# Linear attention and a gated MLP on one core: the order of the readers of the key banks, the time at which even query rows are sent, and the number of output buffers

## The chip, the cores and the metric

The kernel runs on one core of a Trainium2 chip. The metric is the device time of one execution in microseconds (us), taken as the median over runs. A core has five engines that run their own instruction streams in order and wait for each other by semaphores: TensorE (PE in the profile, with its weight loads as PEld), VectorE (DVE), ScalarE (ACT), GpSimd (POOL) and SyncE (SP), which here only starts transfers. Transfers run on 16 DMA engines and are started from SP's, POOL's or ACT's queue.

## The reference

Two stages follow each other. The inputs are q, k, v of shape 8 x 8 x 576 x 64 (batch, heads, tokens, head size), a feature matrix w_phi of 64 x 128, and the weights of a gated MLP.

```python
def phi(x):
    proj = np.einsum('bhsd,df->bhsf', x, w_phi)
    proj = proj - np.max(np.abs(proj), axis=-1, keepdims=True)
    return np.concatenate([np.exp(proj), np.exp(-proj)], axis=-1)
q_p, k_p = (phi(q), phi(k))
kv = np.einsum('bhsf,bhsd->bhfd', k_p, v)
z = np.sum(k_p, axis=2)
num = np.einsum('bhsf,bhfd->bhsd', q_p, kv)
den = np.einsum('bhsf,bhf->bhs', q_p, z)[..., None] + 1e-06
x = num / den            # then heads side by side: 8 x 576 x 512

h = np.maximum(x @ w_in, 0.0)                 # 512 -> 1024, halves u and v
v_n = (v - mean(v)) / sqrt(var(v) + 1e-06)    # over the 512 columns of v
v_s = w_spatial @ v_n + b_spatial             # mixes the 576 tokens
out = (u * v_s) @ w_out
```

Each key row needs the exponential of its 128 projections with both signs, and the largest absolute projection of the row. The kernel takes exp(proj) and exp(-proj) of the plain projections, and carries the maximum into the sums by scaling v with exp(-max) and exp(max).

## The kernel before, in words

**Units.** Of a batch's 576 tokens, 512 are "main" tokens and 64 are a "tail". A unit of work is either a pair of heads of one batch with its 512 main tokens (four pairs a batch, 32 in all), or the 64 tail tokens of two batches with all heads (four units). There are 36 units; unit 0 is the first pair, unit 1 the first tail, units 9, 18 and 27 the other tails.

**Steps.** `step(i)` (line 608) writes one step of a software pipeline. In the order of the list ORDER it takes the keys of unit i (`a_keys`, then `a_scale`), its queries (`a_queries`), the attention of unit i-3, the sums of unit i-2 (`a_kv`), the transposed inputs of unit i+1 (`a_transpose`), the query features of unit i-2 (`a_qfeat`), the output of attention of unit i-4 (`a_x_t`) and the transposed query maxima of unit i-1 (`a_max_t`). Between them `fill` takes tasks of the second stage from a queue, as many as a credit of estimated TensorE time allows. When the last pair of a batch is done, `b_tasks` puts that batch's second stage into the queue. What is still in the queue after the last step runs behind it. The scheduler of the language then orders the instructions of each engine by these priorities and its own estimate of times; instructions wrapped in `pin` keep their written order among themselves.

**Keys (line 251).** `by_token` multiplies the transposed keys with w_phi into a bank of PSUM, the memory that TensorE writes: one bank of 128 x 512 numbers for each half of the unit. Of each bank VectorE takes the maxima (`mk`, one instruction of 128x4 from 128x512, line 259) and ScalarE the exponentials (`kf`, two instructions of 128x512, line 262). In the program's waits, an instruction that reads a bank and was written after another engine's reader of that bank waits for that reader. So the exponentials of a half wait for its maxima. `a_scale` (line 279) then takes the exponentials `em` of the maxima on ScalarE (two instructions of 128x8), and scales v by them on GpSimd (`vs`, two instructions of 128x512 and a small one; `vst` for the tails).

**Queries (line 264).** The same projection in two banks, and the maxima `mq` of both on VectorE. GpSimd (VectorE in the first five units) splits mq into a high and a low part `mhl`; a step later `a_max_t` (line 306) transposes that on TensorE. From batch 2 on (`merged`), VectorE puts the 16 transposed rows into the transposed queries themselves, so that one matmul takes projection and maximum together. The transposed queries `qT` of a pair hold odd heads in partitions 64 to 127 and even heads in partitions 0 to 63. The 16 rows of the maxima overwrite rows 0 to 15 for the odd heads; before that, `q_even` (line 223) has sent rows 0 to 63 to another tile `qE`, one of four that units take in turn, by a transfer from SP's queue. The first copy (line 311) waits for that transfer. A second copy (line 312) puts the maxima into `qE`.

**Transposed inputs.** From batch 2 on, `cross` transposes the keys and queries of a whole batch by two DMA transposes in SP's queue, two steps ahead of the batch's first pair.

**Second stage.** `b_v` and `b_ln` make the normalised v half (ScalarE relu, VectorE statistics, GpSimd normalisation `vn`), `b_u` the u half, `b_s` the mixing of tokens with the product on VectorE, `b_o` the last matmul. `o_mm` (line 524) evicts each 128x512 result into an output buffer `ob`, on VectorE and ScalarE in turn; SP sends it out. There are four such buffers, which the first two loads use too.

Of the kernel before, what the change touches and what calls it, by code (L numbers as in the profile page):

```python
# [8 lines left out]
FP32 = mybir.dt.float32  # L9
BF16 = mybir.dt.bfloat16  # L10
AF = mybir.ActivationFunctionType
ALU = mybir.AluOpType
AX = mybir.AxisListType
# [3 lines left out]
def kernel(  # L17
# [15 lines left out]
    nc = tc.nc  # L33

    B, H, S, D = q.shape
    F = w_phi.shape[1]
    DM = moe_w_in.shape[0]
    DFF = moe_w_in.shape[1]
    HALF = DFF // 2
    P = 128  # L40
    KC = DM // P
    NP = H // 2
    NB = 4
# [8 lines left out]
    a1 = ctx.enter_context(tc.tile_pool(name="stage_a", bufs=2))  # L52
    feat = ctx.enter_context(tc.tile_pool(name="feat", bufs=2))
    small = ctx.enter_context(tc.tile_pool(name="small", bufs=3))
    s2 = ctx.enter_context(tc.tile_pool(name="stage_b", bufs=2))
# [4 lines left out]
    def pin(start):  # L60
        return lambda *a, **kw: tc.keep_in_program_order(start(*a, **kw))

    def main_ap(t, b, h0=0, n=H):
        return bass.AP(tensor=t.tensor, offset=t.offset + (b * H + h0) * S * D,
                       ap=[[NB * D, P], [S * D, n], [1, NB * D]])
# [5 lines left out]
    st = {}  # L71
# [43 lines left out]
    alloc(0)  # L115
    first = {}
    for x, t in (("k", k), ("q", q)):
        first[x] = s2.tile([P, 2, NB * D], FP32, tag="ob", name="first", bufs=4)
        pin(nc.sync.dma_start)(out=first[x], in_=main_ap(t, 0, 0, 2))
    ident = cpool.tile([P, P], BF16)  # L120
    make_identity(nc, ident)
# [100 lines left out]

    def q_even(u):
        u["qE"] = qts[u["i"] % len(qts)]
        pin(nc.sync.dma_start)(out=u["qE"][0:D], in_=u["qT"][0:D])

    def a_transpose(u):
        src = st[u["b"]] if u["pair"] else gs[u["g"]]
# [15 lines left out]
    def by_token(xT, half):  # L244
        ps = psum.tile([P, 4, F], FP32, tag="bank", name="ps")
        for x in range(2):
            nc.tensor.matmul(out=ps[:, 2 * x:2 * x + 2, :], lhsT=xT[:, 2 * half + x, :], rhs=wphi2,  # L247
                             start=True, stop=True)
        return ps

    def a_keys(u):

        u["mk"] = small.tile([P, H], FP32, tag="mk", name="mk")
        u["kf"] = feat.tile([P, 2, H, F], BF16, tag="kf" if u["pair"] else "kf_t", name="kf",
                            bufs=4 if u["pair"] else 2)
        for half in range(2):
            pk = by_token(u["kT"], half)
            hs = slice(4 * half, 4 * half + 4)
            nc.vector.tensor_reduce(out=u["mk"][:, hs], in_=pk, axis=AX.X, op=ALU.max,  # L259
                                    apply_absolute_value=True)  # L260
            for s, sc in ((0, 1.0), (1, -1.0)):
                nc.scalar.activation(out=u["kf"][:, s, hs, :], in_=pk, func=AF.Exp, bias=0.0, scale=sc)  # L262

    def a_queries(u):

        m, early = mhl[u["i"] % NM], u["i"] < EARLY
        if not early:
            mq = small.tile([P, H], FP32, tag="mq", name="mq")
        for half in range(2):
            pq = by_token(u["qT"], half)  # L270
            if early and half == 0:
                mq = pq[:, 0, 0:H]
            nc.vector.tensor_reduce(out=mq[:, 4 * half:4 * half + 4], in_=pq, axis=AX.X, op=ALU.max,  # L273
                                    apply_absolute_value=True)
        eng = nc.vector if early else nc.gpsimd
        eng.tensor_copy(out=m[:, 0:H], in_=mq)
        eng.tensor_tensor(out=m[:, H:2 * H], in0=mq, in1=m[:, 0:H], op=ALU.subtract)

    def a_scale(u):
        em = small.tile([P, 2, H], FP32, tag="em" if u["pair"] else "em_t", name="em", bufs=3 if u["pair"] else 1)  # L280
        for s, sc in ((0, -1.0), (1, 1.0)):
            nc.scalar.activation(out=em[:, s, :], in_=u["mk"], func=AF.Exp, bias=0.0, scale=sc)  # L282
        if u["pair"]:
            pj = u["pj"]
            vs = feat.tile([P, 2, H, DA], BF16, tag="vs", name="vs", bufs=4)
            for s in range(2):
                nc.gpsimd.tensor_tensor(out=vs[:, s, :, 0:D], in0=st[u["b"]]["v"][:, pj * H:(pj + 1) * H, :],  # L287
                                        in1=em[:, s, :].unsqueeze(2).to_broadcast([P, H, D]), op=ALU.mult)
            nc.gpsimd.tensor_copy(out=vs[:, :, :, D:DA], in_=em.unsqueeze(3).to_broadcast([P, 2, H, 2]))
            u["vs"] = vs  # L290
        else:
            d = gs[u["g"]]
            d["vs"], d["unit"], d["em"] = vst[u["g"] % 2], u, em
            for bl in range(2 if u["i"] > 1 else 1):
                tail_scale(u["g"], bl)
# [70 lines left out]
    def norm(pn, x, r=slice(0, P)):  # L366
        n = r.stop - r.start
        rc = small.tile([P, 4, 1], FP32, tag="rc", name="rc", bufs=4)
        nc.vector.reciprocal(out=rc[r], in_=pn[r, :, D:D + 1])
        nc.vector.tensor_tensor(out=x, in0=pn[r, :, 0:D], in1=rc[r].to_broadcast([n, 4, D]), op=ALU.mult)  # L370
# [25 lines left out]
    def tail_num(g, bls):  # L396
        d = gs[g]
        qf = d["unit"]["qf"]
        if "xt" not in d:
            d["xt"] = a1.tile([P, H, D], BF16, tag="xt", name="xt")  # L400
        for i in range(2):
            pn = psum.tile([P, 4, DA], FP32, tag="bank", name="pn")
            for y in range(4):
                for bl in bls:
                    r = slice(bl * TL, (bl + 1) * TL)
                    for s in range(2):
                        nc.tensor.matmul(out=pn[r, y, :], lhsT=qf[i][:, s, y, r],
                                         rhs=st[2 * g + bl]["kv"][:, 4 * i + y, s, :],
                                         start=(s == 0), stop=(s == 1))
            r = slice(bls[0] * TL, (bls[-1] + 1) * TL)  # L410
            norm(pn, d["xt"][r, 4 * i:4 * i + 4, :], r)
# [73 lines left out]
    def b_u_tail(g, bls):  # L485
        d = gs[g]
        if "uTt" not in d:
            d["uTt"] = s2.tile([P, KC, P], BF16, tag="uTt", name="uTt")
        r = slice(bls[0] * TL, (bls[-1] + 1) * TL)
        pu = psum.tile([P, KC, P], FP32, tag="bank", name="pu")  # L490
        for dc in range(KC):
            for kc in range(KC):
                nc.tensor.matmul(out=pu[:, dc, r], lhsT=w_in_bf[:, kc, dc * P:(dc + 1) * P],
                                 rhs=d["xTt"][:, kc, r], start=(kc == 0), stop=(kc == KC - 1))
        nc.scalar.activation(out=d["uTt"][:, :, r], in_=pu[:, :, r], func=AF.Relu, bias=0.0, scale=1.0)
# [28 lines left out]
    def o_mm(lhs, r):  # L524
        po = psum.tile([P, DM], FP32, tag="bank", name="po")
        for dc in range(KC):
            nc.tensor.matmul(out=po[r], lhsT=lhs(dc), rhs=w_out_bf[:, dc, :], start=(dc == 0), stop=(dc == KC - 1))  # L527
        ob = s2.tile([P, DM], FP32, tag="ob", name="ob", bufs=4)
        turn[0] ^= 1
        (nc.vector.tensor_copy if turn[0] else nc.scalar.copy)(out=ob[r], in_=po[r])  # L530
        return ob
# [76 lines left out]
    def step(i):  # L608

        if i == 0:  # L610
            a_transpose(units[0])
        for what, share in ORDER:
            for u in units[max(0, i - 5):i + 2]:
                if u["i"] + lag(u, what) != i or (what in ("sums", "attention", "out") and not u["pair"]):
                    continue
                last = u["pair"] and u["pj"] == NP - 1
                if what == "keys":
                    a_keys(u)
                    a_scale(u)
                elif what == "sums":  # L620
                    a_kv(u)
                elif what == "queries":
                    a_queries(u)
                elif what == "next":
                    a_transpose(u)
                elif what == "maxima":
                    a_max_t(u)
                elif what == "out":
                    a_x_t(u)
                    if last:  # L630
                        finish_batch(u, tail_x_t)
                        queue.extend(b_tasks(u["b"]))
                elif what == "features":
                    a_qfeat(u)
                elif what == "attention":
                    a_num(u)
                    if last:
                        finish_batch(u, tail_num)
            fill(share)
# [12 lines left out]
    def at(i, f, *a):  # L652
        io.setdefault(i, []).append(lambda: f(*a))
# [22 lines left out]
    at(7, weights_with_max)  # L676
    for u in units:
        if merged(u):
            at(u["i"], q_even, u)
    for i in range(NU + 4):  # L680
        step(i)
        for f in io.get(i, []):
# [33 lines left out]
```

## Time and profile before

| what | value |
|---|---|
| median of 13 runs | 294.45 us (292.23 to 298.0) |
| the profiled execution's own time | 292.89 us |
| its span, first to last instruction | 291.1 us |
| its granted TensorE clock, mean | 0.987 |
| maxima of keys (line 259), VectorE | 72 instructions, 47.8 us busy |
| exponentials of keys (line 262), ScalarE | 144 instructions, 76.7 us busy |
| exponentials of maxima (line 282), ScalarE | 72 instructions, 13.1 us busy |
| scaled v (line 287), GpSimd | 64 instructions, 65.7 us busy |
| q_even transfers | 24, 64 KB each, 3.2 us to landing (median) |
| full output transfers | 32, 256 KB each, 2.7 us to landing (median) |

The profile gives the busy time of each engine, for groups of instructions by line, and for any stretch of the span. An instruction's own duration is longer than its share of the engine where instructions overlap: four exponentials in a row take 2.06 us from the first start to the last end, while each one lasts about 0.65 us. The waits list says which line stood still, for whose result, how often and how long. The chain of waits goes back from the last instruction through whatever released each step.

### The profile page before, as it was taken

To read this page: it belongs to the slowest core of one execution; us is meant where nothing else is said; L and a number is where in the kernel's file an instruction comes from. 1 tells how busy PE (TensorE), PEld (TensorE's weight loads), DVE (VectorE), ACT (ScalarE), POOL (GpSimd) and SP (SyncE) were. 2 spreads that over 40 slices of the span, in tenths; PEclk is the share of its full clock that TensorE was granted. 3 is DMA by queue.
4 is the path that set the end of the run, shared out by engine and by line. 5 is a ranking of instruction groups with operands and counts; after the bars stand their busy time and mean duration, and the time that the engine had idled before them with its cause. 6 is when DMAs were issued, how large, how long until landed. Compare 5 with 4: busy or idle time off the path is not lost.

```text
span 291.1 us, 7872 instructions
## 1 busy us (share of the span) xinstructions
PE 259.0 (89%) x2974; PEld 171.2 (59%) x2974; DVE 226.0 (78%) x552; ACT 220.4 (76%) x498; POOL 185.5 (64%) x332
## 2 busy tenths in 40 slices
PE   3188899999999799999699999999899989999983
PEld 2067676766656446666557666666566666545441
DVE  5389997966989928899778998888899976654641
ACT  7658998797689917999889787898998865666011
POOL 8579998886336696359879973766769530068100
PEclk9999999999999959999999999999999999999999
DMA  7979999945659299989991899999912005400036
GB/s 194 224 132 159 207 233 205 165 154 72 92 169 170 47 211 161 172 192 192 150 187 30 213 185 178 236 247 207 194 32 56 19 11 182 146 0 1 2 100 225
DMA packets 83626, 41.88 MB, mean 144 GB/s; under 512 B 50626, under 2 KB 78978, under 8 KB 83588
## 3 DMA queue, kind: packets, MB, share of 16 engines
q1 hardware_dynamic: 56100, 29.90, 45.6%
q0 software_dynamic: 27328, 11.41, 32.9%
q8 instruction: 23, 0.38, 0.6%
q14 instruction: 15, 0.12, 0.1%
q10 hardware_dynamic: 160, 0.07, 0.1%
HBM read 32.85 MB, written 9.44 MB: 145 GB/s over the span
## 4 chain that ended last, share of the span: by engine, by line
PE 46%; ACT 17%; DVE 16%; POOL 8%; DMA 7%; issue 4%; SPq 0%; DVEq 0%; POOLq 0%; ACTq 0%
PE ps L502 9%; PE po L527 8%; ACT kf L262 6%; PE pv L428 5%; ACT qf L346 5%; PE pu L481 4%; PE ps L247 4%; DMA q_tl<-in_q_dram 4%; DVE mk L259 4%; PE pv L359 3%; PE pn L379 3%; PE ps L503 2%; DVE mq L273 2%; DMA out_dram<-ob 2%; POOL vst L302 2%
## 5 line engine op out<-in xcount | busy, mean ns | idle before, releaser
L262 ACT ACTIVATE kf<-ps 128x512 bf16<-128x512 f32 x144 | 76.7, 651 | 9.1 <-DVE mk L259 8.7
L287 POOL TENSOR_TENSOR vs<-v_f,em 128x512 bf16<-128x512 f32 x64 | 65.7, 1048 | 27.9 <-ACT em L282 27.5
L346 ACT ACTIVATE qf<-pq 128x512 bf16<-128x512 f32 x128 | 66.9, 634 | 11.0 <-PE pq L325 8.1
L259 DVE TENSOR_REDUCE mk<-ps 128x4 f32<-128x512 f32 x72 | 47.8, 679 | 1.6 <-PE ps L247 0.7
L273 DVE TENSOR_REDUCE mq<-ps 128x4 f32<-128x512 f32 x62 | 40.1, 679 | 1.6 <-PE ps L247 1.4
L502 PE MATMUL ps<-w_spT,vn 128*128 128x512 bf16 x128 | 34.9, 392 | 2.7 <-POOL vn L445 2.4
L505 DVE TENSOR_TENSOR uT<-ps,uT 128x512 bf16<-128x512 f32 x32 | 21.7, 686 | 15.3 <-PE ps L503 15.3
L428 PE MATMUL pv<-w_in_bf,xT 128*128 128x512 bf16 x128 | 31.6, 379 | 0.6 <-DMA xT<-x 0.5
L481 PE MATMUL pu<-xT,w_in_bf 128*128 128x512 bf16 x128 | 31.4, 379 | 0.1
L527 PE MATMUL po<-w_out_bf,uT 128*128 128x512 bf16 x128 | 30.6, 379 | 0.0
L431 DVE BATCH_NORM_STATS2 stats<-vr 128x6 f32<-128x512 bf16 (+1 forms) x37 | 24.7, 682 | 5.8 <-ACT vr L430 5.5
L530 ACT COPY ob<-po 128x512 f32<-128x512 f32 (+1 forms) x18 | 10.5, 603 | 24.0 <-PE po L527 21.2
L379 PEld LDWEIGHTS <-qf 128*128 128x128 bf16 x512 | 21.0, 98 | 8.4 <-ACT qf L346 2.3
L359 PE MATMUL pv<-vs,kf 128*128 128x66 bf16 x512 | 25.1, 195 | 0.9 <-ACT kf L262 0.9
L430 ACT ACTIVATE vr<-pv 128x512 bf16<-128x512 f32 (+1 forms) x37 | 21.8, 627 | 5.4 <-PE pv L428 5.2
L370 DVE TENSOR_TENSOR x<-pn,rc 128x256 bf16<-128x256 f32 x64 | 24.7, 417 | 0.3
L379 PE MATMUL pn<-kv,qf 128*128 128x66 bf16 x512 | 23.3, 195 | 1.6 <-ACT qf L346 1.5
L445 POOL TENSOR_SCALAR vn<-vr,rs 128x512 bf16<-128x512 bf16 x32 | 24.2, 766 | 0.6
L359 PEld LDWEIGHTS <-kf 128*128 128x128 bf16 x512 | 22.4, 99 | 2.7 <-issue 1.9
L302 POOL TENSOR_TENSOR vst<-v_tl,em 64x512 bf16<-64x512 f32 x16 | 16.3, 1038 | 11.0 <-ACT em L282 10.7
L483 ACT ACTIVATE uT<-pu 128x512 bf16<-128x512 f32 x32 | 20.1, 644 | 3.1 <-PE pu L481 3.1
L361 PE MATMUL pv<-vst,kf 128*128 128x66 bf16 x128 | 21.5, 193 | 0.7 <-POOL vst L304 0.7
(128 smaller groups left out, 543.2 us busy)
## 6 DMA issues: line engine op xcount, KB each, us to landing
v_f<-in_v_dram SPq DMA_DIRECT2D x8, 1024.0 KB, 8.7
out_dram<-ob SPq DMA_DIRECT2D x32, 256.0 KB, 2.7
k_bf<-in_k_dram POOLq DMA_DIRECT2D x7, 512.0 KB, 6.7
q_bf<-in_q_dram POOLq DMA_DIRECT2D x7, 512.0 KB, 7.6
qt<-qT_b SPq DMA_DIRECT2D x24, 64.0 KB, 3.2
v_tl<-in_v_dram SPq DMA_DIRECT2D x8, 128.0 KB, 7.7
w_in_bf<-in_moe_w_in_dram POOLq DMA_DIRECT2D x2, 512.0 KB, 8.1
out_dram<-ob SPq DMA_DIRECT2D x8, 128.0 KB, 2.5
```

What stands on the lines that cost most here:

```text
L259: nc.vector.tensor_reduce(out=u["mk"][:, hs], in_=pk, axis=AX.X, op=ALU.max, apply_absolute_value=True)
L262: nc.scalar.activation(out=u["kf"][:, s, hs, :], in_=pk, func=AF.Exp, bias=0.0, scale=sc)
L273: nc.vector.tensor_reduce(out=mq[:, 4 * half:4 * half + 4], in_=pq, axis=AX.X, op=ALU.max, apply_absolute_value=True)
L287: nc.gpsimd.tensor_tensor(out=vs[:, s, :, 0:D], in0=st[u["b"]]["v"][:, pj * H:(pj + 1) * H, :], in1=em[:, s, :].unsqueeze(2).to_broadcast( ...
L346: nc.scalar.activation(out=qf[:, s], in_=pq, func=AF.Exp, bias=0.0, scale=sc)
L359: nc.tensor.matmul(out=pv[:, hh, s, :], lhsT=u["kf"][:, s, 4 * hh + c, :], rhs=u["vs"][:, s, 4 * hh + c, :], start=(c == 0), stop=False)
L370: nc.vector.tensor_tensor(out=x, in0=pn[r, :, 0:D], in1=rc[r].to_broadcast([n, 4, D]), op=ALU.mult)
L379: nc.tensor.matmul(out=pn[:, pos, :], lhsT=u["qf"][hh][:, s, pos, :], rhs=d["kv"][:, 2 * u["pj"] + hh, s, :], start=(s == 0), stop=(s == 1))
L428: nc.tensor.matmul(out=pv[r], lhsT=lhs(kc), rhs=w_in_bf[:, kc, HALF:DFF], start=(kc == 0), stop=(kc == KC - 1))
L481: nc.tensor.matmul(out=pu, lhsT=w_in_bf[:, kc, dc * P:(dc + 1) * P], rhs=d["xT"][:, kc, :], start=(kc == 0), stop=(kc == KC - 1))
L502: nc.tensor.matmul(out=ps, lhsT=d["vn"][:, sp, cs], rhs=w_spT[:, sp, 0:T0], start=(sp == 0), stop=False)
L527: nc.tensor.matmul(out=po[r], lhsT=lhs(dc), rhs=w_out_bf[:, dc, :], start=(dc == 0), stop=(dc == KC - 1))
```

## The change

Four things are changed.

1. **Order of the readers of the key banks.** Both banks are filled first. Then the program has the exponentials of half 0, the maxima of half 1, the exponentials of half 1, and the maxima of half 0. By the waits of the built program, the exponentials of half 0 wait for TensorE alone, the maxima of half 1 for TensorE alone, the exponentials of half 1 for the maxima of half 1, and the maxima of half 0 for the exponentials of half 0.
2. **`a_scale` goes from behind `a_keys` to behind `a_queries`** within the step, and so do its `em` and `vs`.
3. **`q_even` of the second, third and fourth pair of a batch is sent at the end of the step before.** It reads the batch's transposed queries directly.
4. **Five output buffers instead of four.** The tiles `xt` and `uTt` of the tails go from two buffers to one.

```diff
-        first[x] = s2.tile([P, 2, NB * D], FP32, tag="ob", name="first", bufs=4)
+        first[x] = s2.tile([P, 2, NB * D], FP32, tag="ob", name="first", bufs=5)
...
-        pin(nc.sync.dma_start)(out=u["qE"][0:D], in_=u["qT"][0:D])
+        pin(nc.sync.dma_start)(out=u["qE"][0:D], in_=st[u["b"]]["qT"][0:D, 4 * u["pj"]:4 * u["pj"] + 4, :])
...
-        for half in range(2):
-            pk = by_token(u["kT"], half)
-            hs = slice(4 * half, 4 * half + 4)
-            nc.vector.tensor_reduce(out=u["mk"][:, hs], in_=pk, axis=AX.X, op=ALU.max,
+        pk = [by_token(u["kT"], half) for half in range(2)]
+
+        def maxima(half):
+            nc.vector.tensor_reduce(out=u["mk"][:, 4 * half:4 * half + 4], in_=pk[half], axis=AX.X, op=ALU.max,
                                     apply_absolute_value=True)
+
+        def exponentials(half):
             for s, sc in ((0, 1.0), (1, -1.0)):
-                nc.scalar.activation(out=u["kf"][:, s, hs, :], in_=pk, func=AF.Exp, bias=0.0, scale=sc)
+                nc.scalar.activation(out=u["kf"][:, s, 4 * half:4 * half + 4, :], in_=pk[half], func=AF.Exp,
+                                     bias=0.0, scale=sc)
+
+        exponentials(0)
+        maxima(1)
+        exponentials(1)
+        maxima(0)
...
-            d["xt"] = a1.tile([P, H, D], BF16, tag="xt", name="xt")
+            d["xt"] = a1.tile([P, H, D], BF16, tag="xt", name="xt", bufs=1)
...
-            d["uTt"] = s2.tile([P, KC, P], BF16, tag="uTt", name="uTt")
+            d["uTt"] = s2.tile([P, KC, P], BF16, tag="uTt", name="uTt", bufs=1)
...
-        ob = s2.tile([P, DM], FP32, tag="ob", name="ob", bufs=4)
+        ob = s2.tile([P, DM], FP32, tag="ob", name="ob", bufs=5)
...
                     a_keys(u)
-                    a_scale(u)
...
                     a_queries(u)
+                    a_scale(u)
...
-            at(u["i"], q_even, u)
+            at(u["i"] - min(u["pj"], 1), q_even, u)
```

## The prediction, made before the changed kernel was run

> **What bounds the kernel now.** I read the page's busy times first, then busy time by stretch, the waits, and the timelines of VectorE and ScalarE around the keys of some units.
>
> ```profile
> PE 259.0 (89%) x2974; PEld 171.2 (59%) x2974; DVE 226.0 (78%) x552; ACT 220.4 (76%) x498; POOL 185.5 (64%) x332
> PE 46%; ACT 17%; DVE 16%; POOL 8%; DMA 7%; issue 4%; SPq 0%; DVEq 0%; POOLq 0%; ACTq 0%
> ```
>
> The first line is the busy time over the span of 291.1 us, the second the chain that ended last by engine. No engine is full, and the chain moves between four of them: every engine takes its work in a fixed order and waits for the others in turn. So I go by stretches (columns: length, then PE, PEld, DVE, ACT and POOL busy with counts, clock, DMA).
>
> ```profile
> 22.00:50.00 28.00, 24.65 (x361) 19.54 (x360) 26.04 (x75) 25.66 (x60) 26.58 (x42) 1.00 1.34 202
> 110.00:160.00 50.00, 45.91 (x578) 31.60 (x576) 42.14 (x106) 45.78 (x110) 35.74 (x65) 1.00 0.96 155
> 160.00:210.00 50.00, 48.47 (x591) 32.11 (x590) 45.20 (x102) 43.23 (x102) 35.30 (x61) 1.00 1.23 209
> 210.00:235.00 25.00, 24.54 (x290) 16.52 (x289) 24.11 (x55) 22.50 (x54) 17.67 (x35) 1.00 0.20 41
> 235.00:280.00 45.00, 43.09 (x418) 24.44 (x417) 27.02 (x64) 20.27 (x37) 14.01 (x27) 1.00 0.16 54
> ```
>
> Until 50 us VectorE and ScalarE are both above 90%; from 50 to 235 PE, VectorE and ScalarE share the load, and VectorE has 0.9 us free of the last 25; after 235 PE works off the queue alone. What the change goes for are these waits (total, times, longest):
>
> ```profile
> POOL vs L287 <- ACT em L282: 27.5, 13, 4.6
> ACT kf L262 <- DVE mk L259: 8.7, 8, 4.3
> DVE ob L530 <- DMA out_dram<-ob: 3.6, 3, 1.5
> ACT ob L530 <- DMA out_dram<-ob: 2.8, 2, 1.8
> DVE qT_b L311 <- DMA qt<-qT_b: 1.2, 2, 1.0
> ```
>
> ScalarE waits for the key maxima 8.7 us in all, 5.9 of them before 50 us. In 28 of 36 units it does not wait: it is late with older work when the bank is ready. Unit 5 is typical (VectorE, then ScalarE):
>
> ```profile
> 32.07 1.29 DVE L259 TENSOR_REDUCE mk<-ps 128x4 f32<-128x512 f32 x2
> 33.27 1.28 DVE L273 TENSOR_REDUCE mq<-ps 128x4 f32<-128x512 f32 x2
> ...
> 31.20 2.08 ACT L346 ACTIVATE qf<-pq 128x512 bf16<-128x512 f32 x4
> 33.11 2.13 ACT L262 ACTIVATE kf<-ps 128x512 bf16<-128x512 f32 x4
> ```
>
> VectorE has taken both maxima by 33.27, while ScalarE begins the exponentials at 33.11, straight after the features qf.
>
> **The change, part by part.** The sum is made against the profiled execution's own 292.89 us (span 291.1 and 1.79 around it), which is 1.56 below the median of 294.45; the difference goes to the median. What can be told from no change is 0.5%, some 1.5 us.
>
> *Maxima of half 0 behind its exponentials.* No instruction is added; VectorE gets a wait. Two exponentials take 0.48 to the second's start plus 0.65, so 1.13 us. In unit 5 the changed order on VectorE is max(1), a query maximum, max(0): it gets to max(0) at 32.18 (half 1 in the bank) + 2 x 0.6 = 33.38, but the exponentials of half 0 end at 33.11 + 1.13 = 34.24. Stall 0.86. The same for each unit, with ScalarE's start as if it did not wait for maxima: units 9 to 18 give 1.4, 2.8, 0.75, 0, 0, 0.3, 1.0, 0.8, 0.5, 1.1; all of units 8 to 35 give 18.6 us, units 3 to 7 give 3.9. Behind max(0) in VectorE's order are the second query maximum (GpSimd waits for it with mhl, PE's transpose for that), the divisions of attention, and the copies kT and qT that PE's next projections need.
>
> A stall costs nothing where VectorE would have idled, and a VectorE that is late stalls less in the next unit, because ScalarE has caught up meanwhile. Before 50 us there is no idle time to hide in. Walking units 1 to 7 through with the durations above and the changed order: unit 1 delays VectorE by 0.4, but its `em` comes 0.75 sooner (ScalarE starts at 15.6, not 16.34), hence the tail's scaled v and the first sums, so units 2 and 3 are level again; then new idle of 0.3 (unit 5), 0.3 (6) and 0.4 (7) and a carried 0.3 make VectorE 1.3 us late when it writes xTt, for which PE's first second-stage matmul waits. I take +1.3 (ends: 0, if ScalarE runs ahead; 3.9, all stalls).
>
> From 50 us I set the stalls of each stretch against VectorE's idle time there: 1.4 against 3.2 (to 66), 4.9 against 10.8 (to 110), 6.3 against 7.9, 3.8 against 4.8, and 2.3 against 0.9 (210 to 235). Only the last does not fit: +1.4. Ends: 0 (VectorE just runs a phase later) and 18.6 (nothing hidden). I take the low value, since each stall resets the phase.
>
> *Exponentials of half 0 without a wait.* On the chain after 50 us the wait ends ScalarE's idle time at units 22 (0.69) and 30 (0.76), both with ScalarE as the next link: -1.45. Ends: 0, and -3.2, the sum over units 8 to 35. What is late next there is max(1) for the second pair of exponentials, which fits in the 0.96 us of the first.
>
> *`em` and `vs` later.* 72 `em` instructions stay, but follow max(0), and in about half the units one or two evictions (0.48 each) that stood behind them. GpSimd waits for `em` 27.5 us already, and GpSimd is on the chain only with the normalisation (97 to 104 and 128 to 141 us). There the changed order on GpSimd puts three load issues of 0.8 to 0.95 ahead of vn that came behind it, and takes one vs of 2.1 out; VectorE's last statistics before it move behind one more maximum (0.6). Together about +1.0 once at 97 us, the rest hidden by the two steps between vs and its sums. Ends: -0.7 (unit 1's gain over again) and +5.8 (12 waits x 0.48).
>
> *Even query rows sooner.* 18 of 24 transfers move a step up in SP's queue; each takes SP 0.54, ahead of outputs, and in one step of a batch ahead of the next batch's transposes (2.2 and 2.5 at 85.6 and 87.9 us). VectorE's waits of 0.2 and 1.0 are all there is to win: -0.6; ends -1.2 and +1.1 (two issues ahead of an output). SP does not stall for them: the tile they write was last read by features a step earlier.
>
> *Fifth output buffer.* All 6.4 us of its waits lie in the last 8 us:
>
> ```profile
> 279.11 7.07 PE L527 MATMUL po<-w_out_bf,uT 128*128 128x512 bf16 x32
> 283.09 0.69 DVE L530 COPY ob<-po 128x512 f32<-128x512 f32 x1 [1.36 <-DMA out_dram<-ob]
> 286.75 0.69 DVE L530 COPY ob<-po 128x512 f32<-128x512 f32 x1 [0.79 <-DMA out_dram<-ob]
> ```
>
> PE's last matmul ends at 286.18, so the last eviction comes at most 0.55 sooner: -0.5 (ends 0, -0.55). The single xt and uTt are written a whole pair of batches after their last reader: 0.
>
> Sum: 1.3 + 1.4 - 1.45 + 1.0 - 0.6 - 0.5 = +1.15: 294.0 against 292.89, or 295.6 on the median. As a check, all stalls of 22.5 us times VectorE's 16% of the chain are 3.6, against the 2.7 taken.
>
> The Trainium skill's page Perfetto Trace Analysis, section Identifying the Most-Contended Engine, would judge PE by its weight loads rather than its matmuls (59%, not 89%), and so call VectorE at 78% the engine to relieve. This speaks against the change, which gives VectorE waits to spare ScalarE. By the rule every stall would count and the sum would be about +21 us (315); by the chain's 16% it is a few us.
>
> **The rivals.**
>
> *Faster: ScalarE paces the kernel.* From 191 to 221 us the chain is nearly all ScalarE, which no stall of VectorE holds up. If VectorE only runs later in phase, the stall terms are 0.3 in all, ScalarE gets 3.2, the rows 1.2, the buffer 0.5, GpSimd 0: 0.3 - 4.9 = -4.6, so 289.9. For it: 185 to 235 us at 90%. Against it: max(0) also feeds `em`, and kf waits for maxima only 2.8 us after 50 us. It wins where VectorE's lateness stays under about 1 us a step.
>
> *Slower by more: GpSimd late.* If the vn of five batches starts 1.0 late as at 97 us, instead of one, and PE, which waited 6.6 us for vn before, waits with it: 1.15 + 4 = +5.15, so 299.6. For it: PE's clock fell there (0.92 from 66 to 110). Against: from 154 to 190 us the chain is PE's own work.
>
> *Nothing to tell:* stalls and gains hidden alike, buffer alone: 294.0. The built order does follow the edit, so it can't be that the program is unchanged.
>
> **How the numbers follow.** Forecast, coupling costs a little, 294.3 to 298: 0.46, of which 0.14 within 0.5%. Faster rival, 288.5 to 292.9: 0.32. GpSimd rival: 0.12. Nothing to tell: 0.10. So faster 0.32, same 0.24, slower 0.44. The range takes in both rivals: 289.3 to 300.5.
>
> **What would show it.** Right: VectorE's waits list has mk on kf with 8 to 18 us; kf on mk falls below 3; VectorE's busy share from 22 to 50 us falls from 93% to about 89%, and unit 8's keys come about 1.3 us later; `qT_b` on qt goes; no eviction at the end waits over 0.5 for a transfer, and the last comes within 0.2 of PE. Wrong: mk waits under 5 us in all (the scheduler's gap is filled), or they are there and PE's work from 50 to 235 us is not later (cover larger than taken), or GpSimd's waits for `em` fall.

## The result and the profile after

The changed kernel takes 296.43 us (median of 11 runs, 295.78 to 302.44), the kernel before 294.06 us in the same comparisons (48 runs). The ratio is 1.0124 with a 95% interval of 1.0094 to 1.0155: slower by about 3.6 us. (A ratio here takes only the runs within 1.5% of the fastest of their kernel, which in e2 are 4 of 12; the profiled executions of e2 and e5 are not among them.) The forecast was 295.6, slower by 1.15. The profiled execution took 298.84 us (span 297.1), against 292.89 (span 291.1).

Busy time by engine and the chain of waits of the changed kernel:

```profile
PE 255.8 (86%) x2974; PEld 169.8 (57%) x2974; DVE 225.2 (76%) x552; ACT 221.3 (75%) x498; POOL 184.5 (62%) x332
PE 47%; ACT 19%; DVE 11%; DMA 9%; POOL 8%; issue 4%; POOLq 0%; DVEq 0%; ACTq 0%
```

No engine has more instructions than before; VectorE's share of the chain fell from 16% to 11%, while ScalarE's rose from 17% to 19% and the transfers' from 7% to 9%. The stretches of the changed kernel (length, then PE, PEld, DVE, ACT and POOL busy with counts, granted clock, DMA share and rate):

```profile
22.00:50.00 28.00, 22.26 (x365) 18.78 (x364) 26.02 (x74) 25.30 (x61) 27.43 (x43) 1.00 1.21 189
210.00:235.00 25.00, 22.52 (x271) 15.16 (x270) 20.27 (x48) 21.55 (x51) 18.33 (x36) 1.00 0.50 85
235.00:280.00 45.00, 43.74 (x430) 25.36 (x427) 29.78 (x73) 25.37 (x51) 17.23 (x32) 1.00 0.17 57
```

From 235 to 280 us ScalarE has 25.4 us to do where it had 20.3: work arrives there late. Fixed stretches hold other units than before, though. For the same work, from the first key matmul of unit 3 to that of unit 8, first before, then after the change:

```profile
22.97:48.24 25.27, 21.99 (x338) 17.83 (x339) 23.31 (x69) 24.07 (x58) 24.79 (x39) 1.00 1.34 209
```

```profile
24.91:52.19 27.28, 22.12 (x337) 17.75 (x338) 23.74 (x69) 24.53 (x58) 24.53 (x39) 1.00 1.36 208
```

The same 69 instructions of VectorE fill 92% of 25.27 us before and 87% of 27.28 us after. The waits of the changed kernel (total, times, longest):

```profile
POOL vs L295 <- ACT em L290: 37.1, 12, 6.5
...
DVE mq L281 <- PE ps L247: 9.7, 9, 3.2
...
PE ps L510 <- POOL vn L453: 4.5, 1, 4.5
DVE mk L259 <- ACT kf L264: 4.3, 7, 2.4
...
ACT em L290 <- DVE mk L259: 4.1, 5, 2.3
```

The 8.7 us in which ScalarE waited for maxima are gone (0.2 are left), and with them VectorE's waits for output transfers and for the sent query rows. In their place VectorE waits 4.3 us for exponentials, ScalarE 4.1 us for the maxima that `em` needs, GpSimd 9.6 us more for the `em` of its `vs` (and 4.4 less for that of the tails' `vst`), and PE's 2.4 us of waiting for `vn` in two pieces have become 4.5 us in one.

To see where the time went I compare, in each trace, when PE starts the key projections of a unit. Each column is the length of a stretch (from one unit's keys to another's) minus that of the kernel before; the first is the start of unit 3, the last runs from unit 35 to the end of the span. All are worked out from times in one trace for each kernel (e1 to e13 are the experiments below), in us.

| kernel | to u3 | 3 to 8 | 8 to 15 | 15 to 16 | 16 to 29 | 29 to 30 | 30 to 35 | 35 to end |
|---|---|---|---|---|---|---|---|---|
| changed | +1.93 | +2.02 | +1.24 | +0.04 | -0.12 | 0.00 | +1.22 | -0.37 |
| e1, readers alone | +1.94 | +2.01 | +1.92 | +0.08 | +1.88 | +5.22 | -1.25 | +0.24 |
| e2, scale step alone | +1.56 | -0.04 | -0.11 | -1.00 | +2.01 | +4.52 | -1.23 | +0.80 |
| e3, query rows alone | +2.18 | -0.02 | -0.20 | -0.96 | +0.14 | 0.00 | +0.32 | -0.21 |
| e4, buffers alone | +1.09 | -0.02 | -0.07 | -0.07 | +1.19 | 0.00 | +1.79 | -0.55 |
| e10, readers and scale | +3.16 | +2.07 | +1.77 | +0.10 | +0.41 | +4.45 | -1.25 | +0.12 |
| e5, all but the readers | +2.55 | -0.02 | -0.19 | -2.59 | +0.94 | +0.41 | +1.62 | -0.92 |
| e6, unit 0 old | +0.99 | +1.69 | +1.28 | +0.51 | +1.82 | +0.01 | -0.21 | -0.46 |
| e7, units 0 to 7 old | +2.42 | +0.10 | +1.26 | -0.08 | -0.08 | +0.01 | -0.17 | -0.37 |
| e9, units 8 to 35 old | -1.02 | +2.03 | -0.19 | -2.58 | -0.45 | +0.41 | -1.22 | -0.69 |
| e11, units 8 to 12 old | +3.71 | +1.85 | +0.16 | +1.06 | -0.12 | 0.00 | +0.69 | -0.35 |
| e12, units 13 to 16 old | +1.37 | +2.02 | +0.95 | -1.04 | -0.83 | 0.00 | +0.65 | -0.14 |
| e13, units 17 to 35 old | +1.08 | +1.99 | +1.25 | +0.39 | +1.16 | +0.40 | -0.53 | -0.63 |

The first column belongs to the run, not to the change: e9, e11, e12, e13 and the changed kernel have the same order of readers in units 0 to 7, and their unit 3 starts up to 4.7 us apart. Most of that is the arrival of the first loads: the tail's queries land at 13.60 us in e9, 14.42 in the kernel before, 16.35 in the changed one and 16.52 in e11, and in each the keys of unit 1 start 0.52 us behind that. So 1.9 of the 6.0 us between the two profiled spans are not the change's.

**Units 3 to 8: +2.0.** The `mk` waits make 0.9 us of it; the rest is behind them. PE waits 1.6 us there for the divisions `x` (0.3 in e7, where these units have the old order), which stand behind the maximum of half 0 in VectorE's order.

**Units 8 to 15: +1.24.** It is one stall, in unit 10. VectorE, ScalarE and PE of the changed kernel:

```profile
68.56 0.69 DVE L259 TENSOR_REDUCE mk<-ps 128x4 f32<-128x512 f32 x1
71.68 0.69 DVE L259 TENSOR_REDUCE mk<-ps 128x4 f32<-128x512 f32 x1 [2.43 <-ACT kf L264]
...
68.70 2.00 ACT L354 ACTIVATE qf<-pq 128x512 bf16<-128x512 f32 x4
70.61 2.00 ACT L264 ACTIVATE kf<-ps 128x512 bf16<-128x512 f32 x4
...
72.43 0.30 PE L367 MATMUL pv<-vs,kf 128*128 128x66 bf16 x4 [1.27 <-DVE mk L259]
```

ScalarE works off older features until 70.61, so the maximum of half 0 comes 2.43 us after VectorE was free. PE then waits 1.27 us for that instruction. These matmuls do not read its maxima (they are the sums of an older unit), so I take it that they wait for the bank whose last reader it is; no run shows that by itself.

**Unit 15 to 16: +0.04, where 2.6 us less are to be had.** GpSimd of the changed kernel, and PE behind it:

```profile
102.05 2.04 POOL L295 TENSOR_TENSOR vs<-v_f,em 128x512 bf16<-128x512 f32 x2
104.18 0.24 POOL L446 TENSOR_SCALAR var<-mv 128x4 f32<-128x4 f32 x1
...
104.63 0.80 POOL L61 DMA_DIRECT2D k_tl<-in_k_dram  x1
105.46 1.06 POOL L447 TENSOR_TENSOR rs<-var,neghalf 128x4 f32<-128x4 f32 x1
106.47 0.74 POOL L61 DMA_DIRECT2D k_tl<-in_k_dram  x1
107.24 0.22 POOL L448 TENSOR_TENSOR var<-mv,rs 128x4 f32<-128x4 f32 x1
107.38 0.94 POOL L61 DMA_DIRECT2D k_bf<-in_k_dram  x1
108.35 0.28 POOL L449 TENSOR_SCALAR rs<-var 128x4 f32<-128x4 f32 x1
108.73 3.02 POOL L453 TENSOR_SCALAR vn<-vr,rs 128x512 bf16<-128x512 bf16 x4
...
109.55 0.61 PE L510 MATMUL ps<-w_spT,vn 128*128 128x512 bf16 x1 [4.53 <-POOL vn L453]
```

Three issues, 2.48 us in all, stand between the statistics and `vn`. Before, they came behind it:

```profile
98.48 2.09 POOL L287 TENSOR_TENSOR vs<-v_f,em 128x512 bf16<-128x512 f32 x2
...
101.07 3.01 POOL L445 TENSOR_SCALAR vn<-vr,rs 128x512 bf16<-128x512 bf16 x4
...
104.20 1.52 POOL L61 DMA_DIRECT2D k_tl<-in_k_dram  x2
105.70 0.93 POOL L61 DMA_DIRECT2D k_bf<-in_k_dram  x1
...
101.89 0.39 PE L502 MATMUL ps<-w_spT,vn 128*128 128x512 bf16 x1 [2.01 <-POOL vn L445]
```

From the end of VectorE's last `mv` to the start of `vn` it was 4.29 us before (from 96.78) and is 6.36 now (from 102.37), while that `mv` itself is only 0.4 us later against the keys of unit 15. So it is GpSimd's order, far more than VectorE's lateness, that makes `vn` late. PE idles 4.5 us in one piece. Yet against the kernel before the stretch is no longer, because that one paid at this place with PE's clock. Before (granted clock in the third column from the right):

```profile
100.00:104.00 4.00, 1.60 (x3) 0.30 (x3) 1.58 (x3) 2.92 (x9) 4.00 (x8) 0.79 0.66 155
104.00:108.00 4.00, 3.86 (x41) 2.72 (x42) 1.60 (x5) 0.38 (x1) 4.00 (x7) 0.50 1.18 234
108.00:112.00 4.00, 4.00 (x26) 2.11 (x24) 2.54 (x6) 2.45 (x6) 3.48 (x7) 0.85 1.36 155
```

and the changed kernel:

```profile
108.00:112.00 4.00, 2.45 (x20) 1.50 (x21) 0.20 (x2) 0.00 (x0) 3.78 (x8) 0.66 1.16 290
112.00:116.00 4.00, 4.00 (x44) 2.52 (x43) 2.93 (x7) 1.59 (x4) 4.00 (x7) 0.92 1.07 152
```

The clock was 0.50 in a full stretch before, and recovers sooner after the change. In shorter windows it is 1.00 or 0.50 and nothing between: 0.50 for 6.83 us before (102.34 to 109.17) and for 3.41 us after (109.25 to 112.66). That hid the price of the later `vn`; the experiments uncover it. Sorted by the time at 0.50, the table gives two prices in this stretch. With 3.41 us at 0.50, PE's wait of 4.53 us (changed) costs 1.08 us more than one of 1.75 (e12); with 6.83 us, it costs 1.06 more (e11 against the kernel before). And 3.41 us at 0.50 (e12) cost about 1.5 us against none (e5, e9). So of the 2.6 us some 1.1 are the late `vn`'s and the rest the clock's.

**Units 30 to 35: +1.22.** PE waits 2.11 us for a transposed `x` there. Other kernels with and without the new order have anything from -1.25 (e1) to +1.62 (e5) at this place, so I assign it to no part of the change.

**The end.** Five buffers: the last eviction and the last matmuls of the changed kernel.

```profile
292.80 0.69 DVE L538 COPY ob<-po 128x512 f32<-128x512 f32 x1 [1.04 <-PE po L535]
...
285.63 7.07 PE L535 MATMUL po<-w_out_bf,uT 128*128 128x512 bf16 x32
```

The matmuls end at 292.70, the eviction starts 0.1 later, and waits for PE alone.

### The profile page after: what moved, and what is told of

Its sections match the earlier page's. It is cut to its first block, busy times and chain, and to the rows that moved or that the text cites. A ratio compares the mean times of both kernels' runs of the same rounds, so it can differ in the third digit from the quotient of the medians.

```text
span 297.1 us, 7857 instructions
## 1 busy us (share of the span) xinstructions
PE 255.8 (86%) x2974; PEld 169.8 (57%) x2974; DVE 225.2 (76%) x552; ACT 221.3 (75%) x498; POOL 184.5 (62%) x332
## 4 chain that ended last, share of the span: by engine, by line
PE 47%; ACT 19%; DVE 11%; DMA 9%; POOL 8%; issue 4%; POOLq 0%; DVEq 0%; ACTq 0%
PE po L535 11%; PE pv L436 8%; ACT qf L354 7%; PE ps L510 7%; ACT kf L264 7%; PE ps L247 4%; DMA k_tl<-in_k_dram 4%; DMA xT<-x 3%; DVE mq L281 3%; PE pv L367 3%; DVE mk L259 3%; PE pu L489 3%; PE pn L387 2%; DMA qt<-qT_b 2%; PE ps L511 2%
## 5 line engine op out<-in xcount | busy, mean ns | idle before, releaser
L259 DVE TENSOR_REDUCE mk<-ps 128x4 f32<-128x512 f32 x72 | 48.9, 682 | 7.9 <-ACT kf L264 4.3
L281 DVE TENSOR_REDUCE mq<-ps 128x4 f32<-128x512 f32 x62 | 41.4, 682 | 9.9 <-PE ps L247 9.7
L510 PE MATMUL ps<-w_spT,vn 128*128 128x512 bf16 x128 | 34.2, 386 | 4.8 <-POOL vn L453 4.5
L538 ACT COPY ob<-po 128x512 f32<-128x512 f32 (+1 forms) x18 | 11.1, 618 | 25.1 <-PE po L535 25.1
L438 ACT ACTIVATE vr<-pv 128x512 bf16<-128x512 f32 (+1 forms) x37 | 22.6, 631 | 7.3 <-PE pv L436 6.8
L367 PE MATMUL pv<-vs,kf 128*128 128x66 bf16 x512 | 24.5, 194 | 2.0 <-DVE mk L259 1.6
L367 PEld LDWEIGHTS <-kf 128*128 128x128 bf16 x512 | 21.7, 97 | 4.9 <-DVE mk L259 1.9
L510 PEld LDWEIGHTS <-vn 128*128 128x128 bf16 x128 | 12.0, 98 | 15.6 <-POOL vn L453 4.8
```

Source lines behind the costliest of these rows:

```text
L259: nc.vector.tensor_reduce(out=u["mk"][:, 4 * half:4 * half + 4], in_=pk[half], axis=AX.X, op=ALU.max, apply_absolute_value=True)
L367: nc.tensor.matmul(out=pv[:, hh, s, :], lhsT=u["kf"][:, s, 4 * hh + c, :], rhs=u["vs"][:, s, 4 * hh + c, :], start=(c == 0), stop=False)
L510: nc.tensor.matmul(out=ps, lhsT=d["vn"][:, sp, cs], rhs=w_spT[:, sp, 0:T0], start=(sp == 0), stop=False)
```

## The experiments

Theory at the start: the new order of readers costs, through VectorE standing at the maximum of half 0. Rivals: the scale step moved later costs (GpSimd), or the order costs nothing and the transfers or buffers do. All ratios are to the kernel before, with 95% intervals.

**e1: the order of readers alone.** The kernel before with the new functions `maxima` and `exponentials`:

```diff
-        for half in range(2):
-            pk = by_token(u["kT"], half)
...
+        exponentials(0)
+        maxima(1)
+        exponentials(1)
+        maxima(0)
```

> Reader order alone, a_scale still behind a_keys, the rest as before. If the reader order is the cause (VectorE's wait for max(0) in each unit, and in unit 0 max(0) standing behind a copy that waits for the tail's load), this kernel is 2 to 5 us slower than before, with mk on kf in VectorE's waits and unit 0's em 3 us later. If the later a_scale is the cause, it stays within 1 us of before.

Measured: 303.64 us, ratio 1.0299 (1.0245 to 1.0353). The order alone costs more than twice what the whole change does. Of its waits:

```profile
POOL vs L295 <- ACT em L290: 45.8, 15, 6.5
...
DVE ob L538 <- DMA out_dram<-ob: 9.4, 5, 4.8
DVE mk L259 <- ACT kf L264: 5.2, 8, 2.4
ACT em L290 <- DVE mk L259: 5.2, 6, 2.7
```

New is a wait of 4.8 us of VectorE for an output buffer at unit 30, in the middle of the kernel (+5.22 in the table), where the kernel before has none.

**e2: the move of the scale step alone.**

```diff
                     a_keys(u)
-                    a_scale(u)
...
                     a_queries(u)
+                    a_scale(u)
```

> a_scale behind a_queries alone. If GpSimd being late is the cause, 2 to 5 us slower and GpSimd's waits for em above 33 us. If the reader order is the cause, within 1 us of before.

Measured: 295.22 us, the median of 12 runs from 290.56 to 299.37, where the kernel before has 294.63; the ratio 0.9917 (0.9872 to 0.9963) rests on the four shortest. So whether the move gains by itself stays open; the 2 to 5 us that a late GpSimd was to cost are not there. The trace is that of the longest run. In it VectorE waits 4.6 us for an output buffer between units 29 and 30 (+4.52 in the table), and 4.1 us two evictions sooner; whether the shorter runs have these waits it can't tell:

```profile
DVE ob L530 <- DMA out_dram<-ob: 8.7, 2, 4.6
```

**e3: the query rows sooner, alone.**

```diff
-            at(u["i"], q_even, u)
+            at(u["i"] - min(u["pj"], 1), q_even, u)
```

> Even query rows a step sooner alone. My term: 0.6 us faster, VectorE's wait of qT_b for qt gone. If moving them ahead of transposes and outputs in SP's queue is a cost (as PE's 2.1 us wait for xT at 210 us in the changed kernel's profile could be), 1 us slower or more and a wait of PE for xT near 200 us.

Measured: 293.86 us, ratio 0.9974 (0.9942 to 1.0006). It fits the -0.6 us of the prediction (-0.26% is 0.8 us), and can't be told from nothing.

**e4: the buffers alone.**

```diff
-        ob = s2.tile([P, DM], FP32, tag="ob", name="ob", bufs=4)
+        ob = s2.tile([P, DM], FP32, tag="ob", name="ob", bufs=5)
```

(with `first`, `xt` and `uTt` as in the change)

> Five output buffers, one xt and one uTt, alone. My term: 0.5 us faster (0 to 0.55), no eviction at the end waits more than 0.5 us for a transfer. If the single xt or uTt costs anything, slower, with ScalarE or VectorE waiting for PE at the tails.

Measured: 295.31 us, ratio 1.0015 (0.9981 to 1.0049): nothing.

**e5: the change without the order of readers.** The changed kernel with the old loop of `a_keys`:

```diff
-        exponentials(0)
-        maxima(1)
-        exponentials(1)
-        maxima(0)
+        for half in range(2):
+            pk = by_token(u["kT"], half)
...
```

> The changed kernel with the old order of the readers. If the reader order alone makes the change slow, this is 1 to 3 us faster than before and 4 to 6 us faster than the changed kernel. If the other parts share the blame, it is no faster than before.

Measured: 290.2 us, ratio 0.9891 (0.9851 to 0.9931), faster than both kernels. The three other parts gain 1.1% together (alone 0.8, by e2's four shortest runs, 0.3 and -0.15), and the order of readers takes 2.3% on top of them.

The next six kernels are mixtures: the changed kernel, but with the old order of readers in the units named by a condition in `a_keys`.

```diff
+        if CONDITION:
+            for half in range(2):
+                pk = by_token(u["kT"], half)
...
+            return
         pk = [by_token(u["kT"], half) for half in range(2)]
```

**e6: `u["i"] == 0`.** In unit 0 of the changed kernel the maximum of half 0 stands behind a copy that waits for the tail's load, and `em` comes at 15.04 us, not 11.75.

> The changed kernel with the old order of the readers in unit 0 only. In the changed kernel's profile max(0) of unit 0 stands behind a copy that waits for the tail's load, so em comes at 15.0 us, not 11.8, and GpSimd's vst at 20.5, not 18.6. If that start is a cost, 1 to 2 us faster than the changed kernel. If it is hidden by the load, as the times of unit 3's projections say (1.93 us later than before, as unit 1's), within 1 us of it.

Measured: 295.99 us, ratio 1.0116 (1.0065 to 1.0167), as the changed kernel. That delay lies beside the loads.

**e7: `u["i"] < 8`.**

> The changed kernel with the old order in units 0 to 7. If the stalls before 50 us are what is left of the cost, some 2 us faster than the changed kernel, so near before; unit 8's projections then come no later against unit 1's than before. If the cost lies in the later units, no faster than the changed kernel.

Measured: 294.5 us, ratio 1.0046 (1.0011 to 1.0081), and the 2.0 us between units 3 and 8 are 0.1. So with the late units new, the early ones cost 0.8% of the 2.3.

**e9: `u["i"] >= 8`.**

> The changed kernel with the old order from unit 8 on. If the stalls are hidden after 50 us but for some 1.4 us, it is 1 to 2 us faster than the changed kernel and keeps the 2 us of the early units. If the later units cost more than that, 3 us or more faster than the changed kernel.

Measured: 290.39 us, ratio 0.9904 (0.9865 to 0.9943), again faster than both kernels. The late units cost 2.2% with the early ones new, or 1.55% (from e5 to e7) with them old. Against the changed kernel e9's trace saves 1.43 between units 8 and 15, 2.62 from 15 to 16, and 2.44 from 30 to 35. The early units alone (e5 to e9) cost only 0.1%, though the trace has their 2.03 us. Where e9 gets them back isn't settled.

At `vn`, where the order of readers is old, GpSimd has no load ahead, PE waits 1.76 us and then 0.36 or 0.37 three times, and the clock stays up:

```profile
100.00:104.00 4.00, 1.51 (x17) 0.62 (x12) 2.28 (x4) 3.87 (x10) 4.00 (x8) 1.00 0.65 143
104.00:108.00 4.00, 3.58 (x54) 2.50 (x56) 1.93 (x6) 0.58 (x2) 3.91 (x9) 1.00 1.22 265
```

**e12: `13 <= u["i"] <= 16`.** These are the units whose maxima and scale steps lie around that `vn`.

> The changed kernel with the old order of readers in units 13 to 16 alone. With it GpSimd has vn of the third second stage ahead of the issues of three loads, as in the kernel before. If those issues (0.80, 0.74 and 0.94 us) and PE's slower clock behind its wait are the price of the changed order at this place: 2.6 us faster than the changed kernel, ratio to the kernel before about 1.003, PE's wait for vn there falls from 4.5 to about 2 us. If the lateness of VectorE is the price, and the issues only lie where it shows: within 0.5 us of the changed kernel, 1.011 to 1.012.

Measured: 294.97 us, ratio 1.0042 (1.0009 to 1.0074): 0.8% or 2.4 us less than the changed kernel, as foreseen if GpSimd's order is the price. GpSimd and PE of e12:

```profile
105.14 3.02 POOL L462 TENSOR_SCALAR vn<-vr,rs 128x512 bf16<-128x512 bf16 x4
...
108.42 1.52 POOL L61 DMA_DIRECT2D k_tl<-in_k_dram  x2
109.90 0.94 POOL L61 DMA_DIRECT2D k_bf<-in_k_dram  x1
...
105.96 0.39 PE L519 MATMUL ps<-w_spT,vn 128*128 128x512 bf16 x1 [1.75 <-POOL vn L462]
```

The issues are behind `vn` again, `vn` starts 4.13 us after the last `mv`, and PE's longest wait for it falls from 4.5 to 1.75 us. In its trace 1.08 us of the gain is at the place itself, 0.29 ahead of it, and the rest is spread behind it; the clock fell to 0.58 for one stretch here, which e9 was spared.

**e11: `8 <= u["i"] <= 12`.** This takes out the stall of unit 10.

> The changed kernel with the old order of readers in units 8 to 12 alone. In the changed kernel's trace the keys of unit 12 are 1.3 us later than those of unit 10 against the kernel before, VectorE standing 2.43 us before the maximum of half 0 in unit 10 and PE 1.27 us for the bank that this maximum reads last. If that stall is a price of its own: this kernel is 1.3 us faster than the changed one, ratio to the kernel before 1.0124 - 0.0044 = 1.008, and the keys of unit 12 come 1.3 us sooner against those of unit 8. If the phase only shifts and PE waits elsewhere instead: as the changed kernel, 1.012. GpSimd still has three load issues ahead of vn at 105 us here, so that cost stays by both.

Measured: 296.6 us, ratio 1.0115 (1.006 to 1.017), as the changed kernel. The stall does go, with its 1.1 us between units 8 and 15, but the next stretch takes 1.02 more than in the changed kernel: PE meets the same 4.53 us wait for `vn`, and the clock is low for two stretches instead of one (at 0.50 for 6.83 us instead of 3.41):

```profile
108.00:112.00 4.00, 1.91 (x15) 1.07 (x16) 0.18 (x1) 0.39 (x3) 3.87 (x6) 0.57 1.03 276
112.00:116.00 4.00, 4.00 (x35) 2.42 (x34) 1.51 (x4) 0.38 (x1) 3.91 (x8) 0.57 1.28 173
```

So the stall in unit 10 has a price in the trace, but not one that the time shows. Whether the clock would answer that way in each execution, one trace can't say.

**e13: `u["i"] >= 17`.**

> The changed kernel with the old order of readers in units 17 to 35. The prediction had put its one uncovered stall after 50 us here (1.4 us, 210 to 235) and the gain of ScalarE at units 22 and 30 (1.45). If the places add up (whole late part 2.2%, 1.3 us at units 8 to 12, 2.6 us at 13 to 16): 2 to 2.6 us faster than the changed kernel, ratio 1.004 to 1.006. If the late part costs only at the two earlier places: as the changed kernel, 1.011 to 1.013. If the prediction's two terms here cancel: also as the changed kernel.

Measured: 300.23 us, ratio 1.0199 (1.0148 to 1.025). Neither reading foresaw this: with the old order from unit 17 on the kernel isn't faster than the changed one but slower by 0.75%, where the intervals just overlap. The profiled execution (297.99) is among the shortest of its six runs and shows +1.28 between units 16 and 29 and -1.75 from 30 to 35 against the changed kernel. The +1.28 can't be put down to the order: 1.67 us lie between units 21 and 22, where the clock is at 0.50 from 150.17 to 153.58 us, behind a wait of PE of 1.4 us for `xTt` that the changed kernel has too without its clock falling. The trace of e6, which has the changed kernel's order there, has the same 3.41 us at 0.50 and +1.61. So what makes the six runs longer stays open. The places do not add up: together (e9) the units from 8 on gain 2.2%, and apart they gain 0.1% (e11) and 0.8% (e12) and lose 0.75% (e13). That it depends on where the units before have left the engines is argued, not shown.

**e10: order of readers and scale step, with old rows and four buffers.**

```diff
+        exponentials(0)
+        maxima(1)
+        exponentials(1)
+        maxima(0)
...
                     a_keys(u)
-                    a_scale(u)
...
                     a_queries(u)
+                    a_scale(u)
```

> The kernel before with the order of readers and the move of the scale step, but with the old query rows and four output buffers. The order alone cost 3.0%, with the other three parts around it 2.3%; the scale step alone gained 0.8%. If the scale step is what takes the sting out (ScalarE's wait for the maxima of half 0 in em, 5.2 us with the order alone): ratio 1.010 to 1.017, near the changed kernel, em's wait for mk under 4 us. If the five buffers do it (VectorE stood 4.8 us at unit 30 for an output buffer with the order alone): 1.022 to 1.032, and that wait is there again.

Measured: 303.55 us, ratio 1.0317 (1.0278 to 1.0356), as e1. The scale step doesn't soften the order of readers: GpSimd's waits for `em` fall from 45.8 to 37.3 us, and no time comes of it. VectorE and PE of e10 at unit 30:

```profile
203.11 0.69 DVE L538 COPY ob<-po 128x512 f32<-128x512 f32 x1 [4.09 <-DMA out_dram<-ob]
...
203.86 1.01 PE L247 MATMUL ps<-wphi,qT_b 128*128 128x256 bf16 x4 [2.89 <-DVE ob L538]
```

VectorE stands 4.09 us for a free output buffer, and PE 2.89 us behind it. With five buffers the eviction at this unit does not wait. From e10 to the changed kernel 1.9% are gained, by rows and buffers; the rows were changed along, so the run isn't the buffer's alone, but the wait that goes is the buffer's, 4.45 us in the table.

## Why the prediction was right, and where its steps failed

The direction was right, and the mechanism of the forecast in part: VectorE's waits at the maximum of half 0 take the place of ScalarE's. But a price as large as any other found, the late `vn` (2.4 us in e12), is not such a wait, and the ratio puts the cost at 3.6 us, not 1.15. That the sum came so near is luck, for its errors had both signs: the order of readers stood in it with 1.25 us (1.3 + 1.4 - 1.45) and costs 2.3%, or 6.8 us, with the other parts (8.8 alone), while these stood in it with -0.1 and gain 1.1%, or 3.2 us, together. Nor does the range say much, as it held both rivals too.

- *Maxima of half 0, before 50 us, +1.3.* Measured: +2.0 between units 3 and 8 (0.1 in e7), so by the trace the term was mis-sized by 0.7; in time these units cost 0.8% (e7) or 0.1% (e9). The direct stalls are smaller than in the walk; in unit 5, where 0.86 was worked out, there are none in the changed kernel:

```profile
35.01 0.69 DVE L259 TENSOR_REDUCE mk<-ps 128x4 f32<-128x512 f32 x1 [0.18 <-PE ps L247]
35.61 0.68 DVE L281 TENSOR_REDUCE mq<-ps 128x4 f32<-128x512 f32 x1
36.31 0.69 DVE L259 TENSOR_REDUCE mk<-ps 128x4 f32<-128x512 f32 x1
...
35.17 2.08 ACT L264 ACTIVATE kf<-ps 128x512 bf16<-128x512 f32 x4
```

  ScalarE has its exponentials of half 0 in time. The work behind was named but not priced: the divisions come later, and PE waits for them.
- *The same from 50 us on, +1.4 at 210 to 235.* This step failed as to place. The profile has no loss there: units 32 to 35 take 0.17 us less. It has +1.24 between units 8 and 15, where the prediction had set 4.9 us of stalls against 10.8 us of idle time and called them hidden. Idle time in the same stretch is no cover: the stall in unit 10 is 2.43 us (2.8 worked out), directly ahead of an instruction that PE waits 1.27 us for. The time of e11 does not show its price; in e11's trace the next stretch, with `vn` and the clock, takes it back.
- *Sizes of the stalls.* 22.5 us were worked out if ScalarE's times stayed, and 4.3 us are in the waits list. The prediction had given 8 to 18 as a sign of being right and under 5 as a sign of being wrong, so by its own sign this step failed. ScalarE starts sooner in the changed order (in unit 5 before VectorE gets to the maximum of half 0), as the low ends of the terms had allowed.
- *Exponentials of half 0 without a wait, -1.45.* This step failed. The waits are gone from the list, but units 21 to 23 take 0.2 us less and units 29 to 31 the same as before. Taking a wait off one engine gave the time to the next wait: `em` on the maxima, 4.1 us in all, and VectorE's query maxima on PE, 9.7 us, of which the kernel before had 1.4.
- *`em` and `vs` later, +1.0 at 97 us.* The place and mechanism were right, the three issues ahead of `vn` are in the trace; but the part of the change named as its cause was wrong, and the size. The scale step doesn't bring the issues there: in e2's trace they come behind `vn`, and e1, without it, has the wait, of 4.58 us. The order of readers in units 13 to 16 does, and it costs 2.4 us (e12), 1.1 of them at this place in the trace. The term had one `vs` of 2.1 us go from ahead of `vn`; a `vs` of 2.04 still stands there, at 102.05.
- *Query rows, -0.6.* e3's -0.26% agrees within its interval. DVE's waits for `qt` are gone, as foreseen.
- *Fifth buffer, -0.5; `xt` and `uTt`, 0.* Alone it is nothing (e4), and at the end of the changed kernel it does what was said. Its worth with the other edits was missed: with four buffers, VectorE stalls by 4.1 to 4.8 us at unit 30 in the traces with the order of readers (e1, e10) or the scale step (e2). The prediction took the waits of the kernel before for all that a fifth buffer could save.
- *VectorE's share from 22 to 50 us, "about 89%".* In that stretch it is 93% as before, because other units lie in it. For the same units it fell from 92% to 87%.
- *The rivals.* The one with ScalarE as the pace-maker is refuted: with the order of readers undone the kernel reaches 290.2, and with it alone 303.64. "GpSimd late in five batches" has the right mechanism at one batch instead of five; the 6.6 us that it gives as PE's waits for `vn` add the matmuls' 2.4 and the weight loads' 4.2, which lie at the same places. "Nothing to tell" is outside the interval.
- The Trainium skill, page Perfetto Trace Analysis, section Identifying the Most-Contended Engine, calls for judging PE by its weight loads, and thus had VectorE to relieve. That was right about the sign. That every stall then counts is the prediction's own step, not the page's, and its estimate of 315 us is far above e1's 303.64, the kernel with the most of these stalls (5.2 us).

## What to carry to other kernels

When two engines read the same bank in turn, look at what stands behind the last reader in its own queue and at who waits for it (in unit 10, 2.43 us of VectorE and 1.27 of PE behind that). Swapping the readers moves a wait, and the engine that waits less gives the time to the next wait unless nothing else is due. Before taking a stall as covered, look at what PE needs next at that very place, not at the idle time of the stretch, and follow how the scheduler reorders other queues (here three load issues of 2.48 us ahead of a normalisation; the order of readers around them costs 2.4 us of time). Measure the parts of a change apart and in pairs: here three of four parts gain 1.1% together, one costs 2.3%, and a buffer that is worth nothing alone covers a stall of over 4 us that another part would bring.

## What the runs showed of the hardware that was not expected

- PE's granted clock is 1.00 or 0.50 in these traces; a mean between them, as 0.66, is of a stretch that holds both. Within the kernels it stays at 0.50 for 3.41 us or for twice that, and similar waits are answered differently. Behind the waits for the `vn` above, the kernel before (2.01 and 0.36 us) is at 0.50 for 6.83 us, e12 (1.75 and three times about 0.36) for 3.41, and e9 (1.76 and three times about 0.36) not at all; the 4.53 us of the changed kernel and of e11 give 3.41 and 6.83. The Trainium skill, page TensorE: Matmul & The Clock Gate, section What's actually happening, has the clock at half after a free-running window of about 3.4 us without work. Half and lengths of one or two such windows are what the traces show, and a free-running window would go with the spread between e9 and e12, but PE's two waits in the kernel before are 2.4 us in all, less than the window. For reading a pair of profiles: 3.41 us at 0.50 went with 1.5 to 1.7 us more in a stretch with like waits (e12 against e9; e13 against the changed kernel).
- Five kernels with the same order of readers in units 0 to 7 start unit 3 up to 4.7 us apart (-1.0 to +3.7 against the kernel before), with the arrival of the first loads and, in e11, 3.41 us at a clock of 0.50. A profile against a profile carries that, so stretches are to be compared from one unit to another, not from zero.
- An output of 256 KB, which lands in 2.7 us at the median before and 2.9 after, took up to 7.9 us to land between 178 and 212 us in the kernel before, 7.4 in e10 and 8.8 in the changed kernel. Such a landing is what VectorE waits for in e10, so it is what the buffers have to cover there. That the DMA transposes sent ahead in the same queue are the cause (SP is busy with one for up to 4.4 us there) is argued, not shown.
